# A fused long-convolution and MLP kernel: channel halves by parity, the first stage's input loaded by halves of its places, table and mean work moved

## The chip, the cores and the metric

One NeuronCore of one Trainium2 chip runs the whole program. The metric is device microseconds of one execution, less is better. The program is one launch; its engines are TensorE (PE), VectorE (DVE), ScalarE (ACT), GpSimd (POOL) and SyncE (SP). SP issues most transfers, ACT a few; a transfer that ACT issues stands in the same queue as ACT's computing instructions, in order.

## What is computed

A gated long convolution with a residual, then a two-layer MLP with a residual, on 2048 tokens of 512 channels in bf16:

```python
k_shift = sum over t<4 of k_pad[:, t:t+S] * shift_k[:, 3-t]     # 4-tap filter along the tokens
kv = k_shift * v
y  = irfft(rfft(pad(kv)) * rfft(pad(ssm_k)))[:S] + kv * ssm_D   # convolution over 2048 places, per channel
h  = q + layernorm(q) * y
out = h + relu(layernorm(h) @ w1) @ w2                          # w1: 512 x 1376, w2: 1376 x 512
```

## The kernel before

The convolution is done by a transform of length 4096 in two matmul stages, once for ssm_k (into the tile a1k) and once for kv (into a1x), a product of the two, and an inverse in two stages. The 64 x 32 grid of places lies so that 32 partitions hold 32 blocks of 64 places, for each of four row groups of 128 channels (rg 0 to 3). Each row group's 128 channels form two halves d of 64; the halves go through the stages side by side.

**Loads (lines 94 to 163).** `first_channel` gives each half's first channel: half d of row group rg is a block of 64 adjacent channels. `load_rows` brings ssm_k into kfl[32 rg.., g, d, n] with one transfer for each (rg, d): eight of 256 KB, in pieces of 128 bytes. A group g of the first stage takes one channel of each half, so it reads from all eight transfers. SP issues those of rg 0 and 2, ACT those of rg 1 and, later, rg 3. SP then issues four transposing loads of k, six of v, q's first rows (qn0) and w1.

**Tables (lines 184 to 277).** The first stage's small matrix f1w is made from a sine table f1f (two ACT instructions) that is split into a bf16 part and a remainder, and then copied by GpSimd into eight places (`paired`, L254, L257). The second stage's table tab has 32 x 4 x 64 columns; `turns2(i, b)` makes the angles of one quarter (a multiply-add and a mask on DVE), `sines2` their sines on ACT, `negated` a negated copy on GpSimd in blocks of 1024. Slots 0 to 2 of the table are needed by the second stage of ssm_k (`second_k`), slots 1 to 3 by that of kv. `inverse_turns` prepares the inverse's tables on GpSimd, `diagonals` the filter's diagonal matrices wdiag.

**Front stages.** `s1(gb)` is the first stage for eight groups of ssm_k: matmuls into two PSUM tiles, whose two evacuations go to ACT ("A") and DVE ("D") as its letters say. `tap(u)` filters k with four diagonal matmuls and evacuates to ksh. `second_k(kp)` is the second stage for two of 32 rows. `row(q)` transposes ksh and multiplies it with v into xfl (`to_rows`, L333 and L335). All PSUM tiles are taken in turn from two pools of two. The x stages (lines 547 to 556) are the first stage for kv, with w1's column means between them: `column_means` (16 matmuls, L408, two ACT copies), `center` (four subtractions from w1 on GpSimd, L414). The statistics of q's first rows (`bn_stats`, `moments`, `norm_rows`) are put between the second stages.

**Products and inverse.** `product(kp)` does the second stage for kv and two products for each of 16 spots: one always on DVE (L580), the other on GpSimd (L585, ten spots) or DVE. Its inputs for GpSimd are copied out of PSUM by ACT into usb, three buffers. The inverse is L614 (matmul), L619 (transpose on DVE), L625 and L627 (rounding on GpSimd and ACT), L646 (last matmuls).

**Gates and MLP.** `gate` and `gate_both` multiply the inverse's result with the normalised q and add q (L683, L684, L668, L670), half d by half d; `half(t, d)` picks the two blocks of 64 channels of a half, 0 and 3 or 1 and 2 of four. w1's rows are loaded in the matching order. `mlp1` is L726 and L762, `mlp2` is L781 and L787, whose output step writes half d back to its blocks.

The order of the work on each engine is the order of the program text: nothing is reordered.

Of the kernel before, what the change touches and what calls it, by code (L numbers as in the profile page):

```python
# [55 lines left out]
def kernel(  # L56
# [37 lines left out]
    def first_channel(rg, d):  # L94
        return 128 * rg + 64 * (d ^ (rg % 2))


    def half(t, d):
        return t[..., 0:4:3, :] if d == 0 else t[..., 1:3, :]
# [4 lines left out]
    def load_rows(eng, rg):  # L104
        for d in range(2):
            src = bass.AP(tensor=A_ssm_k.tensor, offset=A_ssm_k.offset + S * first_channel(rg, d), ap=[[64, 32], [S, 64], [1, 64]])
            eng.dma_start(out=kfl[32 * rg:32 * rg + 32, :, d, :], in_=src)
# [4 lines left out]
    def load_v(r):  # L112
        for d in range(2) if r % 2 else (0,):
            n = 64 if r % 2 else P
            src = bass.AP(tensor=A_v.tensor, offset=A_v.offset + first_channel(r, d), ap=[[64 * D, 32], [D, 64], [1, n]])
            nc.sync.dma_start(out=vfl[32 * r:32 * r + 32, :, 64 * d:64 * d + n], in_=src)
# [4 lines left out]
    drow = consts.tile([P, 64], BF16, name="drow")  # L121
# [3 lines left out]
    nc.vector.memset(drow2[:], 0.0)  # L125
# [28 lines left out]
    def load_w1():  # L154
        w1_d = B_w1.rearrange("(a e x) f -> e x a f", a=2, e=4)
        for p, e in ((0, 0), (64, 3)):
            nc.sync.dma_start(out=w1[p:p + 64, 0:2], in_=w1_d[e])
        for p, e in ((0, 1), (64, 2)):
            nc.sync.dma_start(out=w1[p:p + 64, 2:4], in_=w1_d[e])
# [41 lines left out]
    for s in range(0, P, 32):  # L201
        odd = s // 32 % 2
        nc.gpsimd.affine_select(out=ind[s:s + 32, :], in_=ind[s:s + 32, :], compare_op=ALU.not_equal, fill=1.0,
                                base=64 * odd, pattern=[[-1, P]], channel_multiplier=-4 if odd else 4)
# [17 lines left out]
    load_rows(nc.scalar, 3)  # L222
# [5 lines left out]

    def turns2(i, b):
        ta = tb[b] if i else early.tile([P, 16, 64], I32, tag="ta", name="ta", bufs=2)[:]  # L230
        _turns(ta, r2, n2c[:], 8192, o2[:, i, b:b + 1])
        return ta

    ta00 = turns2(0, 0)
    ta01 = turns2(0, 1)
    f1hi = consts.tile([P, 64], BF16, name="f1hi")
    f1lo = consts.tile([P, 64], BF16, name="f1lo")
    f1d = early.tile([P, 64], F32, name="f1d")


    tab = tabp.tile([P, 32, 4, 64], F32R, name="tab")
    nc.vector.tensor_copy(out=f1hi[:], in_=f1f[:])
    nc.vector.tensor_tensor(out=f1d[:], in0=f1f[:], in1=f1hi[:], op=ALU.subtract)
    nc.vector.tensor_copy(out=f1lo[:], in_=f1d[:])

    f1w = consts.tile([P, 2, 2, 64], BF16, name="f1w")

    def spikes():
        for rg in range(DC):
            q = slice(32 * rg, 32 * rg + 32)  # L250
            nc.vector.tensor_copy(out=drow2[q, rg % 2, :], in_=drow[q, :])  # L251

    def paired():
        nc.gpsimd.memset(f1w[:], 0.0)  # L254
        for rg in range(DC):
            for i, f in enumerate((f1hi, f1lo)):
                nc.gpsimd.tensor_copy(out=f1w[32 * rg:32 * rg + 32, i, rg % 2, :], in_=f[32 * rg:32 * rg + 32, :])  # L257
# [14 lines left out]
    def sines2(i, b, ta):  # L272
        _sin(tab[:, 16 * i:16 * i + 16, b, :], ta, 8192)

    def negated(i):
        nc.gpsimd.tensor_single_scalar(out=tab[:, 8 * i:8 * i + 8, 2:4, :], in_=tab[:, 8 * i:8 * i + 8, 0:2, :].bitcast(F32),
                                       scalar=-1.0, op=ALU.mult)
# [51 lines left out]
    def to_rows(q, fl):  # L329
        toks = ksh[:].rearrange("p c (a b) -> p (c a) b", b=64)  # L330
        pst = bank2("pst")[:].rearrange("p b n -> p (b n)").bitcast(BF16)
        for i in range(16):
            nc.tensor.transpose(out=pst[:, P * i:P * i + P], in_=toks[:, :, 16 * q + i], identity=ident[:])  # L333
        for d in range(2):
            nc.vector.tensor_tensor(out=fl[:, :, d, 16 * q:16 * q + 16].rearrange("p h i l -> p i h l"),  # L335
                                    in0=pst.rearrange("p (i d h l) -> p i d h l", d=2, h=16, l=4)[:, :, d],
                                    in1=vfl[:, 16 * q:16 * q + 16, 64 * d:64 * d + 64].rearrange("p i (h l) -> p i h l", l=4),
                                    op=ALU.mult)
# [4 lines left out]
    def stage1(data, a_out, gb, engs, spike=False):  # L343

        pss = [bank2("ps1") for _ in range(2)]
# [16 lines left out]
        oc = a_out[:].rearrange("p c k (r g) -> p (c k) r g", r=DC)  # L362
        for h in range(2):
            copy(engs[h], oc[:, :, 2 * h:2 * h + 2, 8 * gb:8 * gb + 8],
# [86 lines left out]
    def norm_rows(q, out, src):  # L451
        for i in range(4):
            t = 4 * q + i
            nc.vector.tensor_scalar(out=out[:, i, :], in0=src[:, i, :], scalar1=mv1[:, t, 0:1],
# [20 lines left out]

    load_k(0)
    load_k(1)
    spikes()
    sines2(0, 0, ta00)
    ta10 = turns2(1, 0)  # L480
    sines2(0, 1, ta01)
    ta11 = turns2(1, 1)
    diagonals()
    paired()
    negated(0)
    negated(1)
    sines2(1, 0, ta10)
    sines2(1, 1, ta11)
    load_k(2)
    load_k(3)  # L490
    load_v(0)
    load_v(2)
    load_x0()
    load_v(1)
    load_v(3)
    load_w1()
    negated(2)
    negated(3)
    inverse_turns()
    warm(13, lhsT=wdiag[:, 0, 0:2].rearrange("p j g -> p (j g)"))  # L500
    s1(0, "AD")
    s1(1, "AD")
    s1(2, "AD")
    tap(0, "A")
    s1(3, "AD")
    s1(4, "AD")
    tap(1, "D")
    s1(5, "AD")
    s1(6, "AD")
    s1(7, "AD")  # L510
    tap(2, "A")
    second_k(0, "A")
    second_k(1, "D")
    second_k(2, "A")
    tap(3, "A")
    second_k(3, "D")
    second_k(4, "A")
    tap(4, "A")
    second_k(5, "D")
    pairs_pool()  # L520
    second_k(6, "A")
    tap(5, "D")
    nc.vector.bn_stats(out=st[:, 0, :], in_=qn0[:, 0, :])
    second_k(7, "A")
    tap(6, "A")
    nc.vector.bn_stats(out=st[:, 1, :], in_=qn0[:, 1, :])
    second_k(8, "A")
    tap(7, "D")
    nc.vector.bn_stats(out=st[:, 2, :], in_=qn0[:, 2, :])
    nc.vector.bn_stats(out=st[:, 3, :], in_=qn0[:, 3, :])  # L530
    moments(mv1, rstd1, 0)
    second_k(9, "A")
    row(0)
    second_k(10, "D")
    norm_rows(0, qn0, qn0)
    second_k(11, "A")
    row(1)
    second_k(12, "A")
    row(2)
    second_k(13, "D")  # L540
    second_k(14, "A")
    row(3)
    second_k(15, "A")
# [3 lines left out]
    for gb in range(8):  # L547
        stage1(lambda g: xfl[:, g // 4, :, :, g % 4], a1x, gb, ("DA", "AD", "AD", "AD", "AA", "AD", "AD", "AD")[gb])
        if gb == 0:
            column_means(0)  # L550
            for n in (0, 1):
                center(n)
        if gb == 2:
            column_means(1)
            for n in (2, 3):
                center(n)
# [103 lines left out]
    def gate_both(q, h):  # L660
# [4 lines left out]
        for d in range(2):  # L665
            part = lambda t: half(t[:, ts].rearrange("p i (a e x) -> p i a e x", a=2, e=4), d)
            hr = hp[q][:, d, ts].rearrange("p i (a e x) -> p i a e x", a=2, e=2)
            nc.vector.tensor_tensor(out=hr, in0=pzs[q, h][:, :, 256 * d:256 * d + 256].rearrange("p i (a e x) -> p i a e x", a=2, e=2),  # L668
                                    in1=part(qn[q][:]), op=ALU.mult)
            nc.vector.tensor_tensor(out=hr, in0=hr, in1=part(xh[q]), op=ALU.add)  # L670
# [4 lines left out]
    def gate(q, d, pool, part=None):  # L675
# [3 lines left out]
        rs = slice(0, 2) if part is None else slice(part, part + 1)  # L679
        of = lambda t: half(t.rearrange("p i (a e x) -> p i a e x", a=2, e=4)[:, :, rs], d)  # L680
        h = hp[q][:, d]
        hr = h.rearrange("p i (a e x) -> p i a e x", a=2, e=2)[:, :, rs]
        nc.vector.tensor_tensor(out=hr, in0=pzs[q, d, part].rearrange("p i (a e x) -> p i a e x", e=2, x=64), in1=of(qn[q][:]), op=ALU.mult)  # L683
        nc.vector.tensor_tensor(out=hr, in0=hr, in1=of(xh[q]), op=ALU.add)  # L684
# [81 lines left out]
    def mlp2(sc):  # L766
        h1T = h1s[sc]
        for i in range(4):
# [4 lines left out]
            of = lambda t, d: half(t.rearrange("p (a e x) -> p a e x", a=2, e=4), d)  # L773
            pair = lambda t: t.rearrange("p (a e x) -> p a e x", a=2, e=2)
            for s in range(parts):
                ps2 = bank()
                for fc in range(NFC):
                    ksz = min(P, DFF - fc * P)
                    lhsT = h1T[:ksz, fc, i * P:(i + 1) * P]
                    if parts == 1:  # L780
                        nc.tensor.matmul(out=ps2[:], lhsT=lhsT, rhs=w2[:ksz, fc, :], start=(fc == 0), stop=(fc == NFC - 1))  # L781
                    else:
# [73 lines left out]
```

## Time and profile before

| | us |
|---|---|
| three runs | 203.0, 203.05, 203.41 (median 203.05) |
| the profiled execution | 203.05, of which the span of the trace 201.3 |
| busy in the span: PE, DVE, ACT, POOL | 172.1, 147.5, 98.0, 90.7 |
| first stage of ssm_k begins to run through | 14.9 |
| last second_k and row before the x stages end | 50.9 |
| products begin, end | 64.4, 92.8 |
| MLP's matmuls run through from | 117.8 |

A line of the timeline gives start, duration, engine, line of the kernel, operation, output and inputs, how many instructions were merged, and in brackets the idle time before and what ended it. A line of the groups gives busy time in all, mean nanoseconds of one, and idle time before the group's instructions. The chain of waits is followed backward from the last instruction: each piece is work, or a wait that nothing in the profile explains ("issue").

### The profile page before, as it was taken

How to read it: one execution, taken by the hardware profiler on the slowest of the kernel's cores; microseconds unless marked ns; L12 is line 12 of the kernel's file. 1: busy time of each engine (PE TensorE's matmuls, PEld its weight loads, DVE VectorE, ACT ScalarE, POOL GpSimd, SP SyncE). 2: the span in 40 equal slices, each digit the busy share in tenths (PEclk: the TensorE clock that was granted, in tenths of full speed). 3: DMA queues.
4: the chain of work that ended last, by engine and by line, in shares of the span. 5: the costliest groups of instructions: out<-in, count | busy, mean ns of one | idle time of the engine just before them, and what ended most of it. 6: DMA issues, size and time to landing. Idle time of an engine off the chain costs nothing.

```text
span 201.3 us, 4078 instructions
## 1 busy us (share of the span) xinstructions
PE 172.1 (86%) x1638; PEld 109.2 (54%) x1643; DVE 147.5 (73%) x259; ACT 98.0 (49%) x112; POOL 90.7 (45%) x108
## 2 busy tenths in 40 slices
PE   0369989899896877778967999999999999999992
PEld 0127866498775666656745654545454444444451
DVE  7957866999557999999999779979977580471142
ACT  0387688924786566522985568102630174026300
POOL 7999983120299699991985720220130011002000
PEclk9999999999999999999999999999999999999999
DMA  8999999960000000005902540312420272120022
GB/s 118 216 233 200 212 205 145 187 146 0 3 3 3 0 5 0 0 3 160 235 22 52 154 129 11 61 37 61 101 47 19 61 83 50 38 54 13 3 54 52
DMA packets 51379, 15.99 MB, mean 79 GB/s; under 512 B 46784, under 2 KB 50208, under 8 KB 51360
## 3 DMA queue, kind: packets, MB, share of 16 engines
q1 hardware_dynamic: 42464, 14.61, 35.8%
q10 hardware_dynamic: 8896, 1.12, 3.6%
q8 instruction: 13, 0.21, 0.4%
q14 instruction: 6, 0.05, 0.1%
HBM read 9.64 MB, written 2.10 MB: 58 GB/s over the span
## 4 chain that ended last, share of the span: by engine, by line
PE 67%; DVE 18%; POOL 4%; ACT 4%; issue 3%; ACTq 2%; DVEq 0%; POOLq 0%
PE m L726 19%; PE m L781 18%; DVE a1x L580 7%; PE ps L358 5%; DVE zs L619 5%; PE ps2k L388 4%; PE u L388 4%; PE pkv L375 3%; PE pst L333 3%; DVE a1k L585 3%; ACT a1x L317 3%; PE pz L646 3%; PE pi L614 2%; PE pz L656 2%; POOL f1w L257 2%
## 5 line engine op out<-in xcount | busy, mean ns | idle before, releaser
L762 ACT ACTIVATE h1T<-m 128x512 bf16<-128x512 f32 (+1 forms) x44 | 25.9, 598 | 43.5 <-PE m L726 43.5
L726 PE MATMUL m<-hT,w 128*128 128x512 bf16 (+1 forms) x176 | 39.0, 379 | 0.2 <-ACT hT L693 0.2
L781 PE MATMUL m<-w,h1T 128*128 128x512 bf16 (+1 forms) x161 | 36.1, 379 | 0.2
L787 DVE SCALAR_TENSOR_TENSOR o<-m,rstd,hp 128x128 bf16<-128x128 f32 (+1 forms) x48 | 15.8, 388 | 25.7 <-PE m L781 24.9
L448 POOL TENSOR_SCALAR rstd<-mv 128x4 f32<-128x4 f32 x8 | 1.8, 231 | 64.4 <-DVE mv L446 64.4
L726 PEld LDWEIGHTS <-w 128*128 128x128 bf16 (+1 forms) x176 | 17.4, 100 | 20.4 <-issue 0.5
L781 PEld LDWEIGHTS <-h1T 128*128 128x128 bf16 (+1 forms) x165 | 16.0, 98 | 19.3 <-issue 0.3
L388 PE MATMUL u<-a1x,tab 64*128 64x256 f32 x256 | 19.7, 291 | 6.4 <-DVE a1k L585 2.4
L585 POOL TENSOR_TENSOR a1k<-usb,a1k 128x1024 fp32r<-128x1024 f32 x10 | 23.7, 2393 | 2.3 <-DVE a1x L580 2.2
L627 ACT CAST a1x<-zs 128x1024 fp32r<-128x1024 f32 (+2 forms) x10 | 17.3, 1730 | 11.1 <-DVE zs L619 11.1
L388 PEld LDWEIGHTS u<-a1x,tab 64*128 64x128 f32 x256 | 16.4, 185 | 9.7 <-DVE a1x L580 4.2
L580 DVE TENSOR_TENSOR a1x<-u,a1k 128x1024 fp32r<-128x1024 f32 x16 | 19.1, 1218 | 2.2 <-PE u L388 2.2
L625 POOL CAST a1x<-zs 128x1024 fp32r<-128x1024 f32 (+1 forms) x8 | 15.7, 1969 | 7.4 <-DVE zs L619 7.4
L619 DVE STREAM_TRANSPOSE zs<-pi 128x1024 f32<-128x1024 f32 x16 | 18.4, 1215 | 0.5 <-PE pi L614 0.5
L414 POOL TENSOR_TENSOR w<-w,wm 128x1376 bf16<-128x1376 bf16 x4 | 11.2, 2844 | 11.3 <-ACT wm L410 11.3
L614 PE MATMUL pi<-a1k,wd 128*128 128x512 f32 x32 | 13.3, 417 | 2.6 <-DVE zs L619 1.5
L579 ACT COPY usb<-u 128x1024 f32<-128x1024 f32 x10 | 10.1, 1016 | 10.3 <-PE u L388 10.3
L317 ACT CAST a1k<-ps2k 128x1024 fp32r<-128x1024 f32 x11 | 11.0, 1027 | 7.1 <-PE ps2k L388 7.0
L614 PE MATMUL pi<-a1x,wd 128*128 128x512 f32 x32 | 12.8, 400 | 0.0
L319 DVE CAST a1k<-ps 128x1024 fp32r<-128x1024 f32 x8 | 9.6, 1222 | 4.4 <-PE ps L358 4.4
L319 DVE CAST a1x<-ps 128x1024 fp32r<-128x1024 f32 x7 | 8.4, 1222 | 5.1 <-PE ps L358 5.1
L421 PE MATMUL warm<-zero,wdiag 128*128 128x512 bf16 x13 | 4.5, 518 | 8.4 <-DVE drow L251 8.4
(116 smaller groups left out, 281.1 us busy)
## 6 DMA issues: line engine op xcount, KB each, us to landing
xall<-in_A_q_dram SPq DMA_DIRECT2D x16, 128.0 KB, 3.3
out_dram<-o SPq DMA_DIRECT2D x62, 32.0 KB, 1.6
w<-in_B_w_dram SPq DMA_DIRECT2D x4, 344.0 KB, 6.1
w<-in_B_w_dram SPq DMA_DIRECT2D x1, 1280.0 KB, 7.7
kfl<-in_A_ssm_k_dram SPq DMA_DIRECT2D x4, 256.0 KB, 5.6
kfl<-in_A_ssm_k_dram ACTq DMA_DIRECT2D x4, 256.0 KB, 6.7
vfl<-in_A_v_dram SPq DMA_DIRECT2D x2, 512.0 KB, 6.7
vfl<-in_A_v_dram SPq DMA_DIRECT2D x4, 256.0 KB, 5.4
```

The source lines that it names most:

```text
L317: nc.scalar.copy(out=o, in_=i)
L319: nc.vector.tensor_copy(out=o, in_=i)
L388: nc.tensor.matmul(out=ps[:, d, 256 * i:256 * i + 256], lhsT=tab[rw, k1, b:b + 2, :].rearrange("p b k -> p (b k)"), rhs=a_in[rw, c, k1, :] ...
L580: nc.vector.tensor_tensor(out=spot(a1x, kp), in0=u2[:], in1=kk.bitcast(F32), op=ALU.mult)
L585: (nc.gpsimd if pool else nc.vector).tensor_tensor(out=kk, in0=(usb if pool else u1)[:], in1=kk.bitcast(F32), op=ALU.mult)
L614: nc.tensor.matmul(out=ps[:, b, :], lhsT=wd[:, m:m + 2, :].rearrange("p b k -> p (b k)"), rhs=src[:, d, 16 * b:16 * b + 16, c0:c0 + 32], s ...
L619: nc.vector.transpose(out=zs[:], in_=ps[:].rearrange("p b (k c) -> p c (b k)", c=32))
L627: nc.scalar.copy(out=o, in_=i)
L726: nc.tensor.matmul(out=ps1[:fsz].rearrange("p (i t) -> p i t", i=4), lhsT=w1[:, c, fc * P:fc * P + fsz], rhs=hT[sc][:, c // 2, :, c % 2, : ...
L762: nc.scalar.activation(out=h1T[:fsz, fc, :], in_=ps1[:fsz], func=ACT.Relu)
L781: nc.tensor.matmul(out=ps2[:], lhsT=lhsT, rhs=w2[:ksz, fc, :], start=(fc == 0), stop=(fc == NFC - 1))
L787: nc.vector.scalar_tensor_tensor(out=of(o[:], d)[:, a], in0=ps[:, a], scalar=rstd2[:, t, :], in1=pair(hp[sc][:, d, i, :])[:, a], op0=ALU.m ...
```

## The change

A half d is now the channels of one parity: channel 2g + d of a row group's 128. So a transfer of 64 adjacent channels holds both halves of 32 groups, and `load_rows(rg, part)` brings the first or the last 32 of 64 groups; four transfers serve s1(0) to s1(3), the other four s1(4) to s1(7). `half` becomes a step of two through the channels, in the row products, the gates and the output step; w1 is loaded as even and odd rows.

f1w and the diagonal term drow2 are made on DVE with masks by row group instead of copies by partition block. The angle tables of i = 1 get their multiply-add on GpSimd, in the tile that i = 0 used, and their mask on DVE; the negations are cut in two, and those that only kv needs come later. Two of v's transfers go to ACT, wsh's load to the end of ACT's first transfers, q's first rows behind v. The first stages of ssm_k run without taps between them. w1's column means and centering come ahead of the x stages, the statistics of q's first rows are taken among and behind the rows, and `norm_rows` of these rows goes to GpSimd. x's first stage swaps blocks of its output (`swap`) so that the order of the channels agrees.

```diff
     def half(t, d):
-        return t[..., 0:4:3, :] if d == 0 else t[..., 1:3, :]
+        return t[..., d::2]
-    def load_rows(eng, rg):
-        for d in range(2):
-            src = bass.AP(..., offset=A_ssm_k.offset + S * first_channel(rg, d), ap=[[64, 32], [S, 64], [1, 64]])
-            eng.dma_start(out=kfl[32 * rg:32 * rg + 32, :, d, :], in_=src)
+    def load_rows(eng, rg, part):
+        src = bass.AP(..., offset=A_ssm_k.offset + S * (128 * rg + 64 * part), ap=[[64, 32], [S, 64], [1, 64]])
+        eng.dma_start(out=kfl[32 * rg:32 * rg + 32, 32 * part:32 * part + 32].rearrange("p g d n -> p (g d) n"), in_=src)
...
-    nc.scalar.dma_start(out=wsh[:], in_=A_shift_k.rearrange("(r p) j -> p r j", p=P))
-    nc.scalar.dma_start(out=drow[0:P:16, :], in_=A_ssm_D.rearrange("(r g) -> r g", g=64))
-    load_rows(nc.scalar, 1)
-    for rg in (0, 2):
-        load_rows(nc.sync, rg)
+    load_rows(nc.scalar, 1, 0)
+    load_rows(nc.sync, 0, 0)
+    nc.scalar.dma_start(out=drow[0:P:16, :], in_=drow_src)
+    load_rows(nc.sync, 2, 0)
+    load_rows(nc.scalar, 3, 0)
+    load_rows(nc.sync, 0, 1)
+    load_rows(nc.sync, 2, 1)
...
-    load_rows(nc.scalar, 3)
+    load_rows(nc.scalar, 1, 1)
+    load_rows(nc.scalar, 3, 1)
+    nc.scalar.dma_start(out=wsh[:], in_=A_shift_k.rearrange("(r p) j -> p r j", p=P))
...
     def turns2(i, b):
+        t = tt[:, b]
+        (nc.gpsimd if i else nc.vector).tensor_scalar(out=t, in0=r2, scalar1=n2c[:], scalar2=o2[:, i, b:b + 1],
+                                                      op0=ALU.mult, op1=ALU.add)
+        if not i:
+            masked(b)
+    def masked(b):
+        nc.vector.tensor_single_scalar(out=tt[:, b], in_=tt[:, b], scalar=8191, op=ALU.bitwise_and)
+    mask = consts.tile([P, 2], F32, name="mask")
+    nc.vector.memset(mask[:], 0.0)
+    for rg in range(DC):
+        nc.vector.memset(mask[32 * rg:32 * rg + 32, rg % 2:rg % 2 + 1], 1.0)
+    def paired():
+        for r in range(2):
+            nc.vector.tensor_scalar(out=f1w[:, 0, r, :], in0=f1f[:], scalar1=mask[:, r:r + 1], scalar2=None, op0=ALU.mult)
+        for r in range(2):
+            nc.vector.scalar_tensor_tensor(out=f1w[:, 1, r, :], in0=f1f[:], scalar=mask[:, r:r + 1], in1=f1w[:, 0, r, :],
+                                           op0=ALU.mult, op1=ALU.subtract)
     def spikes():
+        for r in range(2):
+            nc.vector.tensor_scalar(out=drow2[:, r, :], in0=drow[:, 1::2], scalar1=mask2[:, 1, r:r + 1], scalar2=None, op0=ALU.mult)
+            nc.vector.scalar_tensor_tensor(out=drow2[:, r, :], in0=drow[:, 0::2], scalar=mask2[:, 0, r:r + 1], in1=drow2[:, r, :],
+                                           op0=ALU.mult, op1=ALU.add)
...
-                                    in0=pst.rearrange("p (i d h l) -> p i d h l", d=2, h=16, l=4)[:, :, d],
-                                    in1=vfl[:, 16 * q:16 * q + 16, 64 * d:64 * d + 64].rearrange("p i (h l) -> p i h l", l=4),
+                                    in0=pst.rearrange("p (i h l d) -> p d i h l", d=2, h=16, l=4)[:, d],
+                                    in1=vfl[:, 16 * q:16 * q + 16].rearrange("p i (h l d) -> p d i h l", d=2, l=4)[:, d],
...
     # the order of the front, after
+    turns2(0, 0); paired(); spikes(); turns2(0, 1); sines2(0, 0)
+    load_k(0); load_k(1); load_k(2); load_k(3)
+    inverse_turns(); diagonals(); negated(0, 0); negated(1, 0); turns2(1, 0)
+    warm(22)
+    s1(0, "AD"); s1(1, "AD"); load_v(nc.scalar, 1, 0); s1(2, "AD"); s1(3, "AD"); load_v(nc.scalar, 1, 1)
+    s1(4, "DA"); s1(5, "AD"); s1(6, "AD"); sines2(0, 1); turns2(1, 1)
+    load_v(nc.sync, 0, 0); load_v(nc.sync, 2, 0); load_v(nc.sync, 3, 0); load_v(nc.sync, 3, 1)
+    load_x0(); load_w1(); masked(0)
+    s1(7, "DA"); tap(0, "D"); tap(1, "A"); tap(2, "D"); second_k(0, "A"); sines2(1, 0); masked(1)
+    second_k(1, "D"); tap(3, "A"); second_k(2, "D"); sines2(1, 1)
+    negated(2, 0); negated(3, 0); negated(0, 1); negated(1, 1); negated(2, 1); negated(3, 1)
+    second_k(3, "D"); tap(4, "A"); second_k(4, "D"); second_k(5, "A"); pairs_pool(); tap(5, "D")
+    second_k(6, "A"); second_k(7, "D"); tap(6, "A"); second_k(8, "D"); tap(7, "A"); second_k(9, "D"); second_k(10, "A")
+    row(0); second_k(11, "A"); second_k(12, "A"); row(1); bn_stats(0); second_k(13, "A"); row(2); bn_stats(1)
+    second_k(14, "A"); row(3); bn_stats(2); second_k(15, "A"); bn_stats(3); moments(mv1, rstd1, 0)
+    column_means(0); column_means(1); center(0); center(1); center(2); center(3)
     for gb in range(8):
-        stage1(lambda g: xfl[:, g // 4, :, :, g % 4], a1x, gb, ("DA", "AD", "AD", "AD", "AA", "AD", "AD", "AD")[gb])
+        stage1(lambda g: xfl[:, g // 4, :, :, g % 4], a1x, gb, ("DA", "AD", "AD", "AD", "AA", "AD", "AD", "AD")[gb], swap=4)
         if gb == 0:
-            column_means(0)
...
+            norm_rows(0, qn0, qn0, nc.gpsimd)
...
-        nc.vector.tensor_tensor(out=hr, in0=hr, in1=of(xh[q]), op=ALU.add)
+        nc.vector.tensor_tensor(out=h[:, :, cs], in0=h[:, :, cs], in1=half(xh[q], d)[:, :, cs], op=ALU.add)
...
+                for d in range(2):
+                    nc.vector.scalar_tensor_tensor(out=half(o[:, w * s:w * s + w], d), in0=half(ps2[:, 0:w], d), scalar=rstd2[:, t, :],
+                                                   in1=hp[sc][:, d, i, w // 2 * s:w // 2 * s + w // 2], op0=ALU.mult, op1=ALU.add)
```

The lines of the order are put together several to a line, with bn_stats written short; everything else in the schedule is as in the kernel before. The last token tile's two parts s are halves of 256 adjacent output channels, both parities each, where they were the two halves d.

More of the change, by code (lines that the diff above doesn't have):

```diff
@@ L498 @@
-    negated(3)
-    inverse_turns()
-    warm(13, lhsT=wdiag[:, 0, 0:2].rearrange("p j g -> p (j g)"))
+    inverse_turns()
+    diagonals()
+    negated(0, 0)
+    negated(1, 0)
+    turns2(1, 0)
+    warm(22)
     s1(0, "AD")
     s1(1, "AD")
+    load_v(nc.scalar, 1, 0)
     s1(2, "AD")
-    tap(0, "A")
     s1(3, "AD")
-    s1(4, "AD")
-    tap(1, "D")
+    load_v(nc.scalar, 1, 1)
+    s1(4, "DA")
     s1(5, "AD")
     s1(6, "AD")
-    s1(7, "AD")
-    tap(2, "A")
+    sines2(0, 1)
+    turns2(1, 1)
@@ L512 @@
+    load_v(nc.sync, 0, 0)
+    load_v(nc.sync, 2, 0)
+    load_v(nc.sync, 3, 0)
+    load_v(nc.sync, 3, 1)
+    load_x0()
+    load_w1()
+    masked(0)
+    s1(7, "DA")
+    tap(0, "D")
+    tap(1, "A")
+    tap(2, "D")
     second_k(0, "A")
+    sines2(1, 0)
+    masked(1)
     second_k(1, "D")
-    second_k(2, "A")
     tap(3, "A")
+    second_k(2, "D")
+    sines2(1, 1)
+    negated(2, 0)
+    negated(3, 0)
+    negated(0, 1)
+    negated(1, 1)
+    negated(2, 1)
+    negated(3, 1)
     second_k(3, "D")
-    second_k(4, "A")
@@ L528 @@
-    tap(7, "D")
+    second_k(14, "A")
+    row(3)
     nc.vector.bn_stats(out=st[:, 2, :], in_=qn0[:, 2, :])
+    second_k(15, "A")
     nc.vector.bn_stats(out=st[:, 3, :], in_=qn0[:, 3, :])
     moments(mv1, rstd1, 0)
[L532 to L543, printed above, removed]
+    column_means(0)
+    column_means(1)
+    for n in (0, 1):
+        center(n)
@@ L544 @@
+    for n in (2, 3):
+        center(n)
     pl.pop("front")
@@ L772, in mlp2 @@
             o = mp.tile([P, D], BF16, tag="o", name="o", bufs=4)
[L773 to L774 removed]
+            w = D // parts
             for s in range(parts):
```

149 lines of the change are left out of this document (54 added, 95 removed).

## The prediction

> **What bounds the kernel now.** I read the chain of waits first, for the stages in order. TensorE takes over at 14.9 us and is nearly continuous up to 50 us (first stage, taps, second stage, rows); from 65 to 112 us VectorE sets the pace (products, then the inverse); from 113 us to the end TensorE does (two matmul layers). The front's beginning is this:
>
> ```profile
> 13.45 0.42 POOL f1w L257 x2
> 13.87 1.02 issue
> 14.90 1.05 PE ps L358 x31
> ```
>
> GpSimd's small copies of f1w end at 13.87, and then TensorE waits 1.02 us more for nothing that an engine shows. The transfer view names it: the last of the eight ssm_k loads is issued by ScalarE at 7.78 and takes 7.0 us to land, so 14.8.
>
> ```profile
> 7.78 2.41 ACTq L107 DMA_DIRECT2D kfl<-in_A_ssm_k_dram  x1
> ...
> DMA to landing us min/median/max: 3.1/6.2/7.0
> ```
>
> By the same view the eight land at about 3.8, 6.5, 6.8, 8.0, 9.4, 10.8, 12.0 and 14.8. The fourth is there at 8.0, and that is what a first stage that needs half the places would wait for.
>
> Then the timeline of GpSimd, since the change adds work there:
>
> ```profile
> 54.20 11.23 POOL L414 TENSOR_TENSOR w<-w,wm 128x1376 bf16<-128x1376 bf16 x4 [11.27 <-ACT wm L410]
> 67.06 4.74 POOL L585 TENSOR_TENSOR a1k<-usb,a1k 128x1024 fp32r<-128x1024 f32 x2 [1.63 <-DVE a1x L580]
> ...
> 86.73 4.73 POOL L585 TENSOR_TENSOR a1k<-usb,a1k 128x1024 fp32r<-128x1024 f32 x2 [0.19 <-DVE a1x L580]
> ```
>
> It centres w1 until 65.43, waits 1.63 us, and then makes ten of the sixteen a1k products, 4.74 us for two, with 0.18 us of idle after each pair: VectorE's turn for three spots is 4.92. So in the product stage GpSimd is within 4% of being the bound. Its last product ends at 91.46, VectorE's last lets the inverse go on at 92.37.
>
> Last the groups with shapes kept apart, for prices:
>
> ```profile
> L335 DVE TENSOR_TENSOR xfl<-pst,vfl 128x1024 bf16<-128x1024 bf16 x8 | 5.2, 700 | 0.7 <-PE pst L333 0.7
> L684 DVE TENSOR_TENSOR hp<-hp,xall 128x1024 bf16<-128x1024 bf16 x3 | 2.1, 691 | 0.1
> L683 DVE TENSOR_TENSOR hp<-pz,qn 128x1024 bf16<-128x1024 f32 x1 | 1.2, 1221 | 0.0
> L276 POOL TENSOR_SCALAR tab<-tab 128x1024 fp32r<-128x1024 f32 x4 | 11.0, 2776 | 0.1
> L307 POOL TENSOR_SCALAR rf<-rf,k1o,ofc 128x1024 int32<-128x1024 int32 x1 | 1.2, 1202 | 0.1
> L454 DVE TENSOR_SCALAR qn<-qn,mv,rstd 128x512 bf16<-128x512 bf16 x4 | 1.4, 410 | 0.0
> ```
>
> A VectorE product of 1024 elements takes 0.69 us where all three operands are bf16 in adjacent pairs, and 1.22 where one is f32.
>
> **1. The first stage's start.** Four loads instead of eight: 8.0 (6.9 if the bytes alone counted, 1.05 MB at the 216 GB/s of that stretch from 2 us; 9.4 if the fifth landing counts). On VectorE: o2 ends at 3.95; five memsets (0.1 each) and two small steps (0.15) to 4.8; the first turn table 1.53 (3.88 to 5.41 now) to 6.3; f1f lands at 6.9 now and 0.5 earlier without wsh's issue ahead; the four steps of f1w at 0.2 (L243, L244) to 7.3, four for drow2 to 8.2. So **8.2 instead of 14.9**. The 22 warm matmuls start at 1.1 on zeros; the 13 of now show 0.43 apart for the first eight and 0.21 after, so they end at 7.5, under cover; if all took 0.43 they would end at 10.5, and that is still hidden by the next point.
>
> **2. What is late next.** Stages 0 to 3 (1.45 each) end at 14.0; stage 4 needs the eighth load, 14.3. ScalarE issues its loads and wsh until 10.2, makes the first sine table (1.13) and has eight evacuations (1.02) and two issues of v (0.6 to 2.1 each) to do: stage 7 is through TensorE at 19.5 to 21.1. But VectorE's `masked(0)` is queued ahead of stage 7's evacuation and waits for GpSimd's turns2(1,0). GpSimd's own start ends at 7.2 as now; then inverse_turns 7.0 (24.91 to 31.92 now), diagonals 0.6 + 2.33, two half negations 1.39 each, the turns 1.2 (L307): 21.1, and 0.5 for collisions with VectorE's table steps (the L257 copies cost 0.57 to 0.78 beside them, 0.23 alone): 21.6. wsh now lands behind the eighth load, about 14.4, just as GpSimd reaches it. Mask 0.7, evacuation 1.2, then the bank is free for tap 2 (1.0): **second_k(0) at 24.5 instead of 28.46**.
>
> **3. Up to the rows.** Eleven second_k at 0.62 and five taps at 1.0 come before row(0): 36.3, its transposes 1.65: 38.0. VectorE's share beside it, ten evacuations of 1.2, a mask and the inverse's masks (0.94) from 23.5, ends at 37.1. So **38.0 instead of 41.90**, not 6.7 earlier. v is covered: two of its loads leave SP, its last is issued by about 27.5 and lands 5.5 later, 33; q's first rows and w1 behind it (0.5 and 1.4 MB at the 200 GB/s of that stretch) by 36 and 43, needed at 43 and 46.
>
> **4. The rows.** Now each multiply reads every second element of pst and vfl. The trace has no such read: bounds 0.69 (same line) and 1.22 (f32). I take 1.22: what the f32 rows have in common with it is one wanted element in each four bytes. Four rows of 2.4, 0.45 of waiting for transposes and two statistics of 0.65 between: the last ends at 49.35 (50.85 now); two more statistics and the aggregates, **51.0**. With 0.69 it would be 48.5.
>
> The Trainium skill, VectorE: DVE Perf Modes, section on mode 2×_1P, speaks against the change: two results a cycle need 16-bit operands with a step of one. By it this sum stands; by the row of the same line the time would be that of the first rival.
>
> **5. GpSimd to the products.** The moments stand ahead of center in GpSimd's queue, and they wait for the aggregates: though the column means are there at 48, centering starts at 51.0 + 1.45 (aggregate's end to rstd's end now) = 52.4 and ends at 63.7. Behind it now stand four norm_rows of 512 bf16, which leave VectorE (4 x 0.41). No such row: 0.22 fixed (L448: 231 ns for 4 elements) plus 512 x 0.96 = 0.71 by L307, the same form with two column operands; 0.22 + 512 x 2.5 = 1.5 by L276. I take 0.8, near L307: 66.9. VectorE and TensorE would be ready for the first product at 62.5 (x's stages, rid of 16 mean matmuls and two ScalarE copies, end at 59.9 instead of 64.39). So GpSimd becomes the bound: ten products at 2.37 end at 90.6, **the inverse goes on at 90.7 instead of 92.37: 1.7 us gained**, where VectorE's chain alone would give 87.8.
>
> The Trainium skill, GPSIMD Engine Reference, section 3.1, gives about 2.6 cycles an element at 1.2 GHz as measured. An estimate by it is 1.1 us for 512, 4.4 for the four, and the sum would be 203.5.
>
> **6. Gates and the end.** L684 in gate(0,0) goes from 0.69 to 1.22 amid a full VectorE (+0.53); in gate(0,1,1) from 0.42 to 0.69 on the chain to the turned copy (+0.27); the other gates (8 x 0.27, 2 x 0.53) lie beside TensorE's layers, whose transposes have 5 us and more of slack. Output steps: two of 256 for 128, 128, 256, no dearer; after the last matmul two of 128 (0.61) for one of 256 (0.48): +0.13. Together **+0.9**.
>
> Sum: the profiled execution took 203.05 (span 201.3), which is also the median shown. 203.05 - 1.7 + 0.9 = **202.3**.
>
> **Rivals.**
> - **The strided products keep 0.69.** For: no row shows them dearer. Against: the f32 rows. Centering from 49.9, products from 64.3 to 88.0, no cost at the gates: 203.05 - 4.3 + 0.1 = 198.9.
> - **Slower: norm_rows on GpSimd.** Place: between centering and the first L585. It decides from 0.98 us for one (63.7 + 4n + 23.8 = 92.37 - 0.93). For: L276 and its like, 2.5 ns an element. Against: L307. At 1.5: products end at 93.4, 203.05 + 1.1 + 0.9 = 205.1.
> - **The halves don't land first.** Two queues share the engines, and if the first four loads land with the rest at 14.8, second_k(0) comes at 14.9 + 8 x 1.3 + 3.0 = 28.3, 3.8 later than I say: the inverse at 94.5, 206.1. Against: the fourth landing at 8.0 now.
>
> **Chances.** Forecast 0.45, own range 201.3 to 203.3 (two thirds of a microsecond of error in step 2 or 3 either way, norm_rows 0.71 to 0.95); rivals 0.17, 0.24, 0.14. A difference of 0.2% (0.4 us) is about what a measurement can tell from none. Of the forecast's 0.45 some 0.28 is faster than that, 0.12 within, 0.05 slower; so faster 0.45, same 0.12, slower 0.43. The range, 199.2 to 205.9, leaves out half of the first rival and half of the last.
>
> **What would show it.** First L358 matmuls at about 8.2 and a short stop at stage 4; GpSimd's turns just ahead of VectorE's mask at 21.6; L335's group at 1.22; GpSimd continuous from rstd to its last product, no 0.18 us idles. If GpSimd waits for VectorE in the products, or L335 stays at 0.7, or row(0) comes at 41 or later, the prediction fails at step 5, 4 or 3.

## The result and the profile after

The changed kernel takes 215.17 us (median of four runs, 214.41 to 218.2) where the kernel before took 203.23 beside it: a ratio of 1.0569, 95% interval 1.0517 to 1.0621. One of the four, 218.2, is a slow run, which the ratio leaves out. The forecast was 202.3 with a range up to 205.9. The profiled execution took 214.67, its span is 212.6 where before's was 201.3.

The chain of waits of the changed kernel (start, duration, what), in order of time, shows who sets the front:

```profile
2.23 3.35 SPq L103
5.63 3.92 SPq L103
9.59 9.28 SPq L139
18.92 4.18 SPq L141
...
31.27 2.46 SPq L111
...
40.21 3.74 SPq L156
44.92 2.91 DMA qn<-in_A_q_dram
48.30 2.35 DVE xfl L341 x2
```

Up to 48 us it is SyncE's queue, issuing one load after the other: ssm_k (L103), k (L139, L141), v (L111), q's first rows (L156). By the page's shares its queue has 20% of the chain of the changed kernel; in the kernel before it had none. The first row product starts at 46.0, and its 2.90 us of waiting before it are for v, where 38.0 was forecast and "v is covered".

The queue is slow because the transfers are. In the table by stage (stretch, length, busy time and count of PE, PEld, DVE, ACT, POOL, granted TensorE clock, DMA share, GB/s) this is 4 to 12 and 12 to 20 us of the kernel before:

```profile
4.00:12.00 8.00, 3.57 (x10) 1.38 (x11) 7.69 (x15) 3.58 (x5) 7.56 (x17) 1.00 1.37 209
12.00:20.00 8.00, 6.38 (x143) 4.53 (x142) 4.68 (x5) 5.98 (x7) 7.83 (x8) 1.00 1.29 226
```

And of the changed one:

```profile
4.00:12.00 8.00, 6.77 (x71) 3.55 (x71) 5.72 (x20) 1.52 (x3) 6.92 (x33) 1.00 1.65 132
12.00:20.00 8.00, 3.08 (x65) 2.81 (x60) 2.00 (x3) 3.04 (x4) 2.78 (x5) 0.82 1.55 134
```

The last column fell by 37 and 41%, while the DMA engines are no less busy (1.65 for 1.37). The same bytes in pieces of the same size. In the view of kfl the median from issue to landing is now 8.6 us, the longest 11.7 (6.2 and 7.0 before):

```profile
L103 SPq DMA_DIRECT2D kfl<-in_A_ssm_k_dram x4: 392/2186/3917, 0.7 to 5.6; - x4
...
DMA to landing us min/median/max: 4.8/8.6/11.7
```

ScalarE's timeline shows what slow transfers do to an engine that issues them and also computes; the last line is TensorE's:

```profile
3.80 7.65 ACTq L103 DMA_DIRECT2D kfl<-in_A_ssm_k_dram  x2
11.49 3.96 ACTq L216 DMA_DIRECT2D wsh<-in_A_shift_k_dram  x1
15.50 1.15 ACT L172 ACTIVATE tab<-tt,nbias 128x1024 fp32r<-128x1024 int32 x1 [9.97 <-issue]
```

```profile
17.60 0.61 PE L356 MATMUL ps<-drow,ind 64*128 64x256 bf16 x4 [4.92 <-ACT a1k L323]
```

The issue of the 4 KB of wsh holds the engine for 3.96 us, and the first evacuations of the first stage stand behind it, so TensorE stops for 4.92 us. In the table by stage TensorE is then nearly idle, and granted half its clock after it:

```profile
12.00:17.00 5.00, 0.68 (x25) 0.52 (x19) 1.96 (x2) 1.50 (x2) 2.78 (x5) 1.00 1.68 131
17.00:20.00 3.00, 2.40 (x40) 2.29 (x41) 0.04 (x1) 1.54 (x3) 0.00 (x0) 0.51 1.35 139
```

The Trainium skill, TensorE: Matmul & The Clock Gate, part 1, says that an idle window of about 3.4 us halves the clock; this trace agrees (a stop of 4.92 us, then 0.51). The trace of e5, below, does not quite: there a stop of 2.53 us, from 10.49 to 13.02, was enough, and stages of 1.07 us took up to 1.95 after it. The measurement decides: half the clock can follow a shorter stop.

Then GpSimd's timeline of the changed kernel, against the one shown of before:

```profile
59.24 11.26 POOL L421 TENSOR_TENSOR w<-w,wm 128x1376 bf16<-128x1376 bf16 x4
70.44 8.31 POOL L461 TENSOR_SCALAR qn<-qn,mv,rstd 128x512 bf16<-128x512 bf16 x4
78.68 23.39 POOL L601 TENSOR_TENSOR a1k<-usb,a1k 128x1024 fp32r<-128x1024 f32 x10
```

It is continuous from the centering to the last product, as step 5 said, but the four `norm_rows` take 8.31 us, not 3.2. And the groups with shapes kept apart:

```profile
L341 DVE TENSOR_TENSOR xfl<-pst,vfl 128x1024 bf16<-128x1024 bf16 x8 | 9.3, 1211 | 2.9 <-DMA vfl<-in_A_v_dram 2.9
L461 POOL TENSOR_SCALAR qn<-qn,mv,rstd 128x512 bf16<-128x512 bf16 x4 | 8.3, 2119 | 0.0
L696 DVE TENSOR_TENSOR hp<-hp,xall 128x1024 bf16<-128x1024 bf16 x3 | 3.7, 1225 | 0.1
L696 DVE TENSOR_TENSOR hp<-hp,xall 128x512 bf16<-128x512 bf16 x2 | 1.4, 692 | 0.1
```

The strided products (L341, before L335 at 700 ns) and the gates (L696, before 691 ns) cost 1.21 and 1.22 us, as step 4 had it.

So two things are to be explained: why the loads run at 132 GB/s, and what the price of `norm_rows` is worth.

### The profile page after: what moved, and what is told of

Its sections match the earlier page's. It is cut to its first block, busy times and chain, and to the rows that moved or that the text cites. A ratio compares the mean times of both kernels' runs of the same rounds, so it can differ in the third digit from the quotient of the medians.

```text
span 212.6 us, 4085 instructions
## 1 busy us (share of the span) xinstructions
PE 179.2 (84%) x1652; PEld 114.6 (54%) x1652; DVE 152.7 (72%) x248; ACT 96.0 (45%) x110; POOL 98.7 (46%) x109
## 3 DMA queue, kind: packets, MB, share of 16 engines
q10 hardware_dynamic: 13020, 1.65, 8.5%
## 4 chain that ended last, share of the span: by engine, by line
PE 48%; SPq 20%; DVE 15%; POOL 6%; issue 4%; ACT 3%; DMA 1%; DVEq 0%; POOLq 0%
PE m L790 18%; PE m L738 18%; SPq L141 5%; SPq L111 4%; DVE a1x L596 4%; SPq L139 4%; SPq L103 4%; DVE zs L635 4%; POOL a1k L601 3%; DVE xfl L341 3%; PE pi L630 3%; PE u L395 3%; SPq L156 2%; PE ps L364 2%; PE pz L662 2%
## 5 line engine op out<-in xcount | busy, mean ns | idle before, releaser
L774 ACT ACTIVATE h1T<-m 128x512 bf16<-128x512 f32 (+1 forms) x44 | 25.9, 597 | 43.5 <-PE m L738 43.5
L790 PE MATMUL m<-w,h1T 128*128 128x512 bf16 (+3 forms) x187 | 38.8, 367 | 0.0
L793 DVE SCALAR_TENSOR_TENSOR o<-m,rstd,hp 128x256 bf16<-128x256 f32 (+1 forms) x34 | 14.2, 484 | 24.6 <-PE m L790 24.6
L395 PE MATMUL u<-a1x,tab 64*128 64x256 f32 x256 | 20.7, 306 | 10.0 <-ACT usb L595 4.5
L790 PEld LDWEIGHTS <-h1T 128*128 128x128 bf16 (+1 forms) x187 | 18.1, 98 | 19.8 <-issue 0.3
L395 PEld LDWEIGHTS u<-a1x,tab 64*128 64x128 f32 x256 | 17.7, 201 | 13.0 <-ACT usb L595 4.9
L282 POOL TENSOR_SCALAR tab<-tab 128x512 fp32r<-128x512 f32 x8 | 12.1, 1534 | 4.0 <-ACT tab L172 4.0
L630 PE MATMUL pi<-a1x,wd 128*128 128x512 f32 x32 | 13.7, 428 | 0.0
L323 ACT CAST a1k<-ps2k 128x1024 fp32r<-128x1024 f32 x9 | 9.3, 1042 | 7.6 <-PE ps2k L395 7.4
L395 PE MATMUL ps2k<-a1k,tab 64*128 64x256 f32 x128 | 10.3, 294 | 1.9 <-DVE xfl L341 1.9
L341 DVE TENSOR_TENSOR xfl<-pst,vfl 128x1024 bf16<-128x1024 bf16 x8 | 9.3, 1211 | 2.9 <-DMA vfl<-in_A_v_dram 2.9
```

Source lines behind the costliest of these rows:

```text
L395: nc.tensor.matmul(out=ps[:, d, 256 * i:256 * i + 256], lhsT=tab[rw, k1, b:b + 2, :].rearrange("p b k -> p (b k)"), rhs=a_in[rw, c, k1, :] ...
L630: nc.tensor.matmul(out=ps[:, b, :], lhsT=wd[:, m:m + 2, :].rearrange("p b k -> p (b k)"), rhs=src[:, d, 16 * b:16 * b + 16, c0:c0 + 32], s ...
L774: nc.scalar.activation(out=h1T[:fsz, fc, :], in_=ps1[:fsz], func=ACT.Relu)
L790: nc.tensor.matmul(out=ps2[:, 0:w], lhsT=h1T[:ksz, fc, i * P:(i + 1) * P], rhs=w2[:ksz, fc, w * s:w * s + w], start=(fc == 0), stop=(fc == ...
L793: nc.vector.scalar_tensor_tensor(out=half(o[:, w * s:w * s + w], d), in0=half(ps2[:, 0:w], d), scalar=rstd2[:, t, :], in1=hp[sc][:, d, i, ...
```

## The experiments

**Are adjacent pieces the cause?** The new loads write 256 adjacent bytes as two pieces of 128; the old ones skip 128 bytes after each. e1 gives the kernel before the adjacent form (which gives each group of the first stage other channels, so other values are computed); e2 gives the changed kernel the skipping form.

```diff
e1:
-            eng.dma_start(out=kfl[32 * rg:32 * rg + 32, :, d, :], in_=src)
+            eng.dma_start(out=kfl[32 * rg:32 * rg + 32, 32 * d:32 * d + 32].rearrange("p g e n -> p (g e) n"), in_=src)
e2:
+        for d in range(2):
+            src = bass.AP(..., offset=A_ssm_k.offset + S * (128 * rg + 64 * part + d), ap=[[64, 32], [2 * S, 32], [1, 64]])
+            eng.dma_start(out=kfl[32 * rg:32 * rg + 32, 32 * part:32 * part + 32, d, :], in_=src)
```

> The kernel before, with one thing changed: each of the eight ssm_k transfers writes its 128-byte pieces next to each other in a partition (8 KB in a row) instead of one in every 256 bytes. The channels land permuted, so the output is not the reference's; volume, sources, queues and order are as before. Theory 1 (adjacent 128-byte pieces are written at about 130 GB/s, separated ones at 216): the rate from 3 us on falls to 130 GB/s, the eighth load lands at 18 to 19.5 instead of 14.8, the first stage starts 3 to 5 us later and the time is 206 to 209. Theory 2 (it is the order in which row groups share the two queues): rate 216 GB/s, time 203.05 within 0.4.

> The changed kernel, with each ssm_k load cut into an even and an odd transfer of 128 KB (16 instead of 8), so that the 128-byte pieces of one transfer land 256 bytes apart; the tile is filled as in the changed kernel. Theory 1: 200 GB/s or more up to 12 us, the first four groups' data there at 8 to 9 us, ScalarE free of its issues by 10 to 11, row(0) at 38 to 41 instead of 46 to 48; GpSimd still bounds the products with its 8.3 us of norm_rows, so the inverse goes on at about 96 instead of 102.1: 207 to 210. Theory 2: rate still 130, time 214 to 216.

e1: 202.35 us against 203.41 (ratio 0.9948, 0.9915 to 0.9982), 211 and 223 GB/s in the two stretches; why it is 0.5% faster was not pursued. e2: 213.15 (1.0485, 1.0413 to 1.0557), 147 and 162 GB/s. The theory of adjacent pieces fell on both sides.

**Is it the order of the row groups?** In the changed kernel ACT loads rows 3 early and row 1 late; e3 puts the loads in before's order.

```diff
-    load_rows(nc.sync, 2, 0)
-    load_rows(nc.scalar, 3, 0)
     load_rows(nc.sync, 0, 1)
+    load_rows(nc.scalar, 1, 1)
+    load_rows(nc.sync, 2, 0)
...
-    load_rows(nc.scalar, 1, 1)
+    load_rows(nc.scalar, 3, 0)
```

> The changed kernel with the eight ssm_k loads in the order of before (SP: row group 0, 0, 2, 2; ScalarE: 1, 1, 3, 3); pieces adjacent as in the changed kernel. Theory 1: rate stays at 130 GB/s, the first stage starts later than in the changed kernel since its first half is complete only with the last loads, time 214 to 219. Theory 2: rate back to 200 GB/s and more, time 207 to 211.

One run of 212.51 us, which says little by itself; but 142 and 155 GB/s. This fell too.

**Where the tiles lie.** What was left is the place in SBUF that the transfers write. In the kernel before kfl begins at byte 40192 of each partition, a multiple of 128; in the changed one at 40128, 64 bytes behind one, and vfl behind it likewise. The diff shows why: ahead of them drow grew by 128 bytes, f1hi and f1lo (128 each) went, and mask and mask2 came, 32 each as they are placed: 64 bytes less. e5 puts 64 bytes back; e6 moves the kernel before by 64.

```diff
+    shift = consts.tile([P, 32], BF16, name="shift")
+    nc.vector.memset(shift[:, 0:2], 0.0)
```

> The changed kernel with 64 unused bytes added to the constants, so that ssm_k's and v's tiles start at byte 40192 and 56576 of a partition as in the kernel before, instead of 40128 and 56512 (64 past a multiple of 128). Theory 3 (the small pieces are written slowly because every 128-byte piece lies across a 128-byte boundary): rate 200 GB/s and more from 4 to 12 us, ScalarE's first sine table at 10 to 12 instead of 15.5, row(0) at 37 to 40 instead of 46 to 48, GpSimd's centering from 51 to 54, its norm_rows 8.5 us, its first product at 71 to 74, the inverse at 95 to 98 instead of 102.1: time 207 to 211. Rival (a transfer that only the changed kernel has, or the place of wsh and drow in the queues, slows them): rate 130 to 150, time 213 to 216.

> The kernel before with 64 unused bytes among the constants, so that ssm_k's and v's tiles start 64 bytes past a multiple of 128; nothing else. Theory 3: 130 to 150 GB/s while ssm_k loads, the eighth load lands at 18 to 21 instead of 14.8, v complete at 45 to 48 instead of 37.8, and the time is 207 to 213. Rival: 216 GB/s, 203.05 within 0.5.

e5: 207.44 us (207.11 to 207.77) against 203.71, ratio 1.0183 (1.016 to 1.0205). e6: 211.97, ratio 1.0405 (1.0352 to 1.0458). The first stretch in e5, then in e6:

```profile
4.00:12.00 8.00, 5.87 (x88) 3.72 (x87) 7.48 (x21) 2.87 (x5) 6.89 (x33) 1.00 1.38 218
```

```profile
4.00:12.00 8.00, 3.56 (x9) 1.34 (x10) 7.27 (x15) 1.82 (x3) 7.55 (x17) 1.00 1.60 147
```

64 bytes, and nothing else but one small fill, take the kernel before from 209 to 147 GB/s and give the changed one 218 for 132. (The 64 bytes also move the tiles around these two, w1, kT and ksh; the rate of this stretch is mostly that of ssm_k's loads.) With them e5's front comes within 1.4 us of the forecast: kfl lands in 3.8, 5.7, 6.6 us (min, median, max), and the chain no longer begins in SyncE's queue. GpSimd of e5:

```profile
52.66 11.21 POOL L423 TENSOR_TENSOR w<-w,wm 128x1376 bf16<-128x1376 bf16 x4
63.83 8.29 POOL L463 TENSOR_SCALAR qn<-qn,mv,rstd 128x512 bf16<-128x512 bf16 x4
72.06 23.40 POOL L603 TENSOR_TENSOR a1k<-usb,a1k 128x1024 fp32r<-128x1024 f32 x10
```

Centering at 52.66 (52.4 forecast) to 63.87 (63.7), and from there the loss comes from L463.

**Which offsets, and whose loads?** e10 moves the kernel before by 32 bytes instead of 64 (`[P, 16]` in the tile above). e11 is e5 with 64 bytes between kfl and vfl, so that ssm_k lands on multiples of 128 and v does not.

```diff
+    apart = front.tile([P, 32], BF16, name="apart")
+    nc.vector.memset(apart[:, 0:2], 0.0)
     vfl = front.tile([P, 64, P], BF16, name="vfl")
```

> The kernel before with 32 bytes more in its constants, so that the tiles kfl and vfl begin 32 bytes behind a multiple of 128 instead of 64 (e6) or 0 (before); nothing else differs but one small fill on VectorE. Theory A (a piece of 128 bytes that does not begin at a multiple of 128 is written as two, whatever the offset): 130 to 150 GB/s while ssm_k is loaded and 211 to 213 us, as in e6. Rival B (each further piece that starts off a multiple of 64 costs more still): under 130 GB/s and over 214 us. Rival C (only an offset of 64 hurts): 209 to 218 GB/s and 203 to 204 us.

> e5's kernel (the changed one with kfl and vfl both at multiples of 128 bytes, 207.4 us) with 64 bytes between the two tiles, so that kfl stays at a multiple of 128 and vfl begins 64 bytes behind one. Theory A (the price of the offset is paid while ssm_k is loaded, which the first stage waits for; v has slack of several us before the first row): rate 209 to 218 GB/s over 4 to 12 us, the loads of 512 KB of v 8 us or more from issue to landing instead of 6.5, the first row begins within 0.5 us of e5's 39.0, 207 to 208.5 us. Rival (a good part of the 7.3 us is v's): the first row waits for v and begins past 41, 210 us or more.

e10: 212.3 us, ratio 1.0441 (1.0405 to 1.0477), 144 GB/s: about the same price as at 64, so of the offsets tried it is being off the multiple that costs. e11: 209.54 (208.33 to 209.69), ratio 1.0283 (1.0231 to 1.0334), between the two expectations: 220 GB/s in the first stretch, but 8.8 us for v's loads of 512 KB (6.5 in e5), and the first row waits for its loads:

```profile
40.84 4.62 DVE L345 TENSOR_TENSOR xfl<-pst,vfl 128x1024 bf16<-128x1024 bf16 x4 [3.31 <-DMA qn<-in_A_q_dram]
```

Its transposes had ended at 38.36; it starts at 40.84, 1.8 us later than e5's 39.01. The profile names q's load, which the product does not read; v's last load, issued at 32.38 ahead of it in the same queue, took 8.1 us, to 40.5. So of the 7.7 us between the changed kernel and e5 about 2.1 belongs to v and what lies behind it, more than the slack that I gave it, and the rest to ssm_k. That the 2.1 is v's alone is not shown: kT and ksh move with it, and k's three last loads hold SyncE's queue for 12.95 us in e11, 11.82 in e5.

**The price of `norm_rows`.** e7 undoes nothing and does one part alone: the kernel before with these four instructions on GpSimd, behind the centering (`norm_rows(0, qn0, qn0, nc.gpsimd)` after the last `center`, instead of on VectorE between the rows).

> The kernel before with norm_rows of the first rows moved to GpSimd, behind centering, nothing else. Theory A (2.1 us for one is GpSimd's own price, and GpSimd bounds the products): four norm_rows of 2.1 us from 65.4 to 73.9, the first product at 74 instead of 67.1, ten of 2.37 with no idle, the inverse at 97.5 to 98 instead of 92.4, time 207.5 to 208.7. Rival (the 2.1 us come from work beside it in the changed kernel, or the products have slack): 203 to 205.5.

208.73 us, ratio 1.0246 (1.0215 to 1.0277). GpSimd's timeline in e7:

```profile
53.84 11.20 POOL L414 TENSOR_TENSOR w<-w,wm 128x1376 bf16<-128x1376 bf16 x4 [11.23 <-ACT wm L410]
65.04 8.25 POOL L454 TENSOR_SCALAR qn<-qn,mv,rstd 128x512 bf16<-128x512 bf16 x4
73.26 23.36 POOL L585 TENSOR_TENSOR a1k<-usb,a1k 128x1024 fp32r<-128x1024 f32 x10
```

The first product stands at 73.26 instead of 67.06, 6.2 later: the wait of 1.63 us there covers the first part of the 8.25. The ten products then run without the 0.18 us of idle after each pair, in 23.36 us for 24.40, and 5.2 are left of it; the time is 5.0 longer.

e4 takes the instructions off GpSimd in the changed kernel, back to VectorE, now among x's stages (`if gb == 2: norm_rows(0, qn0, qn0)`).

> The changed kernel with norm_rows of the first rows on VectorE again, behind the third x stage. Theory A (GpSimd's queue bounds the products, and the four norm_rows cost it 8.3 us): GpSimd's first product comes at 70.5 to 71 instead of 78.7; then VectorE's chain bounds, later by 1.4 us of its own norm_rows: the inverse at 96 to 97.5 instead of 102.1, time 209 to 210.5. Theory B (the products wait for something else, the transfers' lateness alone): time 214.7 within 1.

A miss: 218.03 us, 1.0725 (1.0658 to 1.0792), slower still. VectorE and then GpSimd in e4:

```profile
60.43 9.43 DVE L461 TENSOR_SCALAR qn<-qn,mv,rstd 128x512 bf16<-128x512 bf16 x4
```

```profile
58.42 11.29 POOL L421 TENSOR_TENSOR w<-w,wm 128x1376 bf16<-128x1376 bf16 x4
80.36 4.73 POOL L601 TENSOR_TENSOR a1k<-usb,a1k 128x1024 fp32r<-128x1024 f32 x2 [10.65 <-DVE a1x L596]
```

Three of the four take 2.89 us on VectorE; the same instruction takes 0.41 elsewhere in this run. They lie over the centering, whose pieces are 2.82 us: each waits for one of them to end, the evacuations of x's stages wait behind, and GpSimd is idle for 10.65 us afterwards. The Trainium skill, SBUF — State Buffer, in its section on the two separate sides, calls the port pair of these two engines an exclusive lock that is held for a whole instruction; the 2.89 us agree.

So e8 puts them on ScalarE, at product step 14, into e5's kernel: `activation` with rstd as scale and minus mean times rstd (two small GpSimd instructions) as bias.

```diff
-            norm_rows(0, qn0, qn0, nc.gpsimd)
+    def norm_act():
+        for i in range(4):
+            nc.scalar.activation(out=qn0[:, i, :], in_=qn0[:, i, :], func=ACT.Identity, scale=rstd1[:, i, :], bias=nmr[:, i, :])
...
+        14: (norm_act,),
```

> The kernel of e5 with norm_rows on ScalarE, among the last products (four instructions with a scale and a bias of one column each; GpSimd makes the bias, two instructions on 4 elements). Theory A: GpSimd's first product at 64 to 66, VectorE's and GpSimd's chains end within 1.5 us of each other, the inverse at 88.5 to 90.5 instead of 92.4 before; gates 0.9 dearer; time 200 to 202. If e5's gain is not there either, 208 and more.

202.14 us (nine runs, 202.0 to 204.06) against 203.71, ratio 0.9928 (0.9909 to 0.9948): 0.7% less than before. This is a little more than was expected, and the inverse's transposes begin 1.4 us earlier than before (91.76 for 93.12) where 1.9 to 3.9 were expected; the trace is of the longest of the nine runs, 204.06. Four instructions in 2.93 us at 85.99, under the products; the first product on GpSimd at 66.09:

```profile
85.99 2.93 ACT L607 ACTIVATE qn<-qn,shift,rstd 128x512 bf16<-128x512 bf16 x4
```

**What binds then?** e9 is e8 with the column means ahead of second_k(15) and the centering ahead of the moments in GpSimd's queue.

```diff
+    column_means(0)
+    column_means(1)
     second_k(15, "A")
     nc.vector.bn_stats(out=st[:, 3, :], in_=qn0[:, 3, :])
-    moments(mv1, rstd1, 0)
...
+        center(n)
+    moments(mv1, rstd1, 0)
```

> e8's kernel with the two groups of column means issued ahead of second_k(15), and GpSimd's four centering instructions ahead of the four small ones that make rstd1 and the negated mean times rstd1 (only the ScalarE pass at product step 14 reads those). Theory A: GpSimd's queue, full from the first centering to the tenth product, sets the end, so whatever starts it earlier is gained. In e8 the means' copy ended at 50.75 and GpSimd began the moments only at 51.83, centering at 53.75; here the copy should end near 49.5 and centering run 49.5 to 60.7, the first product wait for its ScalarE copy at about 63.5 instead of 66.09, and the inverse begin some 2.5 us earlier: 199.3 to 200.5 us, ratio 0.980 to 0.987. Rival: after the x stages TensorE and VectorE set the pace of the products (VectorE's products wait for TensorE and the other way round), GpSimd then idles between products, and the time stays within 1 us of e8: 201.2 to 202.5 us. Second rival: the means' sixteen matmuls ahead of second_k(15) hold back the first x stage by their 2.5 us, and the time is no better than e8's.

201.81 us (seven runs, 200.9 to 202.45), ratio 0.9926 (0.9895 to 0.9957). The intervals of e8 and e9 overlap, so whether e9 is the faster of the two stays open; the 2.5 us of its first theory are not there. In its trace GpSimd begins the centering at 48.30 (53.75 in e8), then waits:

```profile
64.22 4.75 POOL L603 TENSOR_TENSOR a1k<-usb,a1k 128x1024 fp32r<-128x1024 f32 x2 [2.62 <-DVE a1x L598]
69.14 4.75 POOL L603 TENSOR_TENSOR a1k<-usb,a1k 128x1024 fp32r<-128x1024 f32 x2 [0.17 <-DVE a1x L598]
...
90.28 12.56 DVE L642 STREAM_TRANSPOSE zs<-pi 128x1024 f32<-128x1024 f32 x11 [0.30 <-PE pi L637]
```

2.62 us of idle and then 0.17 after each pair: VectorE sets the pace of the products again, as in the kernel before, and GpSimd's early start is spent in waiting. The inverse's transposes begin at 90.28, 1.5 earlier than e8's 91.76, while x's own stages come only 0.4 earlier; some of the 1.5 may be e8's long execution.

## Why the prediction was wrong, step by step

The loss against the kernel before, by the ratios times 203.4: the offset of the tiles 7.9 us (1.0569 to 1.0183), `norm_rows` on GpSimd, against ScalarE, 5.2 (1.0183 to 0.9928), and a gain of 1.5 from the rest.

**Step 1, the first stage's start: failed at its rate.** The 8.0 for the fourth landing, and "1.05 MB at the 216 GB/s of that stretch" beside it, took the pace of the loads from the trace of before for transfers that the change sends elsewhere. In the changed kernel the eight land between about 5.5 and 19.2 us. The stage starts in pieces at 9.8; the first of these wait for the small load of drow (VectorE waits 1.58 us for it, until 8.64, a landing for which the step has no term), the next for ssm_k. The dearer part comes after: the stop of 4.92 us, because ScalarE is held in its issues until 15.45 where step 2 had it free at 10.2. With the tiles back on a multiple of 128 the stage starts at 8.1 (e5), about the number of the step. So the count of loads and the VectorE steps were right; the offset was not among the unknown costs at all, and no rival held it. "The halves don't land first" priced late loads, but with another mechanism, at 206.1.

**Step 2, what is late next: 1.4 us late in e5, and held by another engine than it says.** second_k(0) comes at 25.9 for 24.5. GpSimd's turns, which the step made the releaser of `masked(0)`, end at 22.70 instead of 21.6, because GpSimd waits 1.31 us for wsh, which "lands just as GpSimd reaches it". But VectorE gets to the mask (L236) only at 23.05, behind an evacuation that had itself waited for TensorE. TensorE and VectorE in e5:

```profile
13.02 0.40 PE L358 MATMUL ps<-drow,ind 64*128 64x256 bf16 x4 [2.53 <-ACT a1k L325]
14.46 1.95 PE L366 MATMUL ps<-f1w,kfl 64*128 64x128 bf16 x32
```

```profile
21.91 1.23 DVE L327 CAST a1k<-ps 128x1024 fp32r<-128x1024 f32 x1 [1.36 <-PE ps L366]
23.05 0.68 DVE L236 TENSOR_SCALAR tt<-tt 128x1024 int32<-128x1024 int32 x1
```

The chain of e5 follows this back to ScalarE, which issues until 10.9, makes its sine table, and begins to evacuate at 11.97. By then two stages have filled the four PSUM tiles, and TensorE stops for 2.53 us and has half its clock for a while (granted 0.72 over 12 to 17 us). The step let stages 0 to 3 end at 14.0 without a stop; by its own figures (10.2, 1.13 and 1.02) the first tile is free only at 12.35. Stage 3 ends at 16.4 and stage 7 at 23.0, where 19.5 to 21.1 was said. In the changed kernel as it stands the step is buried: second_k(0) at 30.9.

**Step 3, up to the rows: right in e5, wrong as it stands.** 39.0 for 38.0 in e5, 1.0 late by step 2's miss. "v is covered" holds only with v's tile on the multiple; in e11, without, the first row is 1.8 us later and the time 2.1 longer.

**Step 4, the rows: right.** 1.22 taken, 1.21 measured; the last row ends at 49.8 in e5 for 49.35. The rule of the Trainium skill, VectorE: DVE Perf Modes, section on mode 2×_1P, that was weighed there, and the f32 row taken for its price, agree with L341; the first rival (0.69 kept, 198.9) fell.

**Step 5, GpSimd to the products: the mechanism right, the size of its term wrong.** GpSimd is the bound and its ten products have no idle left; but one `norm_rows` is 2.12 us, where 0.8 was taken and 0.71 to 1.5 given as bounds. The lower bound came from an int32 row, the upper from one in f32 with another output type; neither was a bound for a bf16 instruction with two column operands. The estimate of 1.1 us by the Trainium skill, GPSIMD Engine Reference, section 3.1, was short of it too. The second rival had this mechanism: put 2.12 into its own sum (63.7 + 4n + 23.8, +0.9 for the gates) and it gives 207.6, 4.5 over the kernel before; e5 measured 207.44, 3.7 over the 203.71 beside it, and its products end at 95.5 where the sum has 96.0. So without the offset the case would have been that rival, with a price outside its bounds.

**Step 6, gates and end: the prices right, the sum not settled.** L696 takes 1.22 and 0.69, as priced. From the first transpose of the inverse to the end of the span it is 108.2 us in before and 109.3 in e7, and with the changed gates 109.5 in e5, 110.2 in e8 and 109.0 in e9. By the pair that is +0.2 (e7, e5: norm_rows on GpSimd in both), +0.8 (before, e9) or +2.0 (before, e8). The +0.9 lies among them, but no run changes the gates alone.

That e8 lands on the forecast's 202.3 is partly chance: it has no `norm_rows` on GpSimd at all, and in its trace second_k(0) is 1.9 and row(0) 1.5 us later than forecast.

## What to carry to other kernels

When a change adds, drops or resizes a tile, add up the bytes ahead of every tile that a transfer with small pieces writes: here 64 bytes cost 7.9 us, where the best of the rivals gained 4.2. An instruction that moves to another engine is priced from a row of the same types on that engine, or with bounds wide enough to say that there is none; and look whether a third engine has room, for here ScalarE took in 2.93 us what cost GpSimd 8.3 and VectorE, beside GpSimd, 9.4.

## What the runs showed of the hardware

- Transfers in pieces of 128 bytes to SBUF ran at 209 to 220 GB/s over 4 to 12 us where the tile began at a multiple of 128 (before, e1, e5, e7, e8, e9, e11) and at 132 to 147 where it began 32 or 64 bytes behind one (after, e2, e3, e4, e6, e10). The starts on the multiple were multiples of 256 too (40192 is 157 times 256); a start 128 behind one was not tried. The Trainium skill, DMA: Bandwidth & Descriptors, in its section on how a descriptor splits, tells of reads that every transaction starts at a multiple of 256. If writes split likewise, which it does not say, every second shifted piece needs two, three for two in all; an estimate by it is 209 / 1.5 = 139 GB/s, near the 147 and 144 of e6 and e10. No run here separates that from another cause.
- A subtract-and-multiply of 512 bf16 with two column operands took 2.07 to 2.12 us on GpSimd in every kernel that has it there, where the negation of 512 f32 (L282 of the changed kernel) took 1.53. Why the bf16 one is the dearer stays open.
- On ScalarE the issue of a 4 KB transfer behind four of 256 KB took 2.37 us (e11) to 3.96 us (after), and all that ScalarE computes waited.
